# Turning a second batch by DMA transposes, and moving the next batch's loads behind its scores, in a fused attention and feed-forward kernel

## The chip, the cores and the metric

The kernel runs on one core of one Trainium2 chip. The metric is the device time of one execution in microseconds (us). "Before" is the kernel without the change, "after" the kernel with it. Because the same kernel's median moves by up to about 1 us between chips and sessions, kernels are compared by the ratio to runs of "before" that were taken in turn with them on the same chip.

In the views, PE is TensorE, PEld its weight loads, DVE is VectorE, ACT ScalarE, POOL GpSimd, and SP the engine that issues the stores and the DMA transposes; a q behind a name means that engine's sequencer. The granted clock is the share of its full clock that TensorE was allowed in a stretch. "To land" is said of a transfer whose last byte has arrived.

## The reference

```python
# q, k, v: (8, 8, 1024, 64); E, F: (64, 1024); float32 in and out
k_proj = einsum('ks,bhsd->bhkd', E, k)
v_proj = einsum('ks,bhsd->bhkd', F, v)
scores = (1 / sqrt(64)) * matmul(q, k_proj.transpose(0, 1, 3, 2))
attn   = softmax(scores)                      # over 64 projected keys
x      = matmul(attn, v_proj)                 # to (8192, 512)
g      = x @ w_gate                           # (8192, 1536)
out    = (g * sigmoid(g) * (x @ w_val)) @ w_out
```

## The kernel before

All large matmuls are bf16. The work is cut into 8 batches of 2 chunks of 512 tokens. A chunk has 12 steps; a step is a gate group (`gps`), a value group (`vps`) and an output group (`yps`) of four 512-wide matmuls each. The attention of the *next* batch is placed between these groups, in numbered slots, two to a step. A unit of attention in a slot is for instance the projection of k and v (`u_KV`), a score group (`u_S`), its sum and reciprocal on VectorE (`u_R`), its multiply on GpSimd (`u_N`), or a product with the projected values (`u_PV`).

Scores need q turned, and the products with v need the attention turned. A turn is either four TensorE transposes and a copy (`u_T`, `u_A`) or, for a whole chunk, one DMA transpose issued from SP (`u_TD`, `u_AD`):

```python
BY_DMA = [(b, ch) for b in range(1, B) for ch in range(CH)][1:]   # batches 1 to 7, but not batch 1, chunk 0
...
    def u_AD(b, ch):
        t = aw.tile([P, 4, NPAIR, P], BF16, name="AT", tag="AT")
        nc.sync.dma_start_transpose(out=..., in_=AA.pop((b, ch, "d"))...)
...
    def load_v(b, heads=(0, H)):          # fp32 in DRAM to bf16 on chip: issued by GpSimd
        ...
            nc.gpsimd.dma_start(out=t[:, h0:h1]..., in_=v[b, h0:h1]...)
```

Batches are counted from 0 in the code; "second batch" is `b == 1`, "third batch" `b == 2`.

The softmax here doesn't subtract the row's maximum and nothing guards it: scores larger than these inputs give would overflow.

## Time and profile before

| | before |
|---|---|
| median us, with the runs taken beside "after" | 573.73 (572.9 to 574.41, 4 runs) |
| span of the profiled execution | 572.4 us |
| TensorE share of the chain that ended last | 94% |
| first feed-forward group starts | 22.57 us |
| steps 12 and 24 start (the first `gps` of the second and third chunk; the second batch's attention lies mostly between them) | 47.72 and 87.03 us |

The prediction shows the lines of the page that carry this. In short: TensorE works almost without a hole from 22.57 us to the end, so time is won only by taking instructions off TensorE, by starting sooner, and it is lost wherever TensorE has to wait.

The third batch's projection, in the timeline of TensorE in the kernel before (start us, us, what):

```profile
87.03 1.03 PE L322 MATMUL gps<-xT,wg 128*128 128x512 bf16 x4
...
88.45 0.38 PE L147 MATMUL kvp<-vb,FT 128*64 128x512 bf16 x1
...
90.06 1.04 PE L322 MATMUL vps<-xT,wv 128*128 128x512 bf16 x3
```

The projection runs from 88.21 to 90.06, 1.85 us.

### The profile page before, as it was taken

What the parts mean: (1) busy time and instruction counts of PE and PEld (TensorE: products, weight loads), DVE (VectorE), ACT (ScalarE), POOL (GpSimd) and SP (SyncE); (2) the same over time, 40 slices, a digit from 0 to 9 for tenths busy, and PEclk for the clock granted to TensorE, in tenths of its full rate; (3) what the DMA queues carried; (4) which work ended last, traced back from release to release, by engine and by line L of the source; (5) the groups of instructions that cost most, each with busy time, mean ns of one, the idle gap of its engine ahead of it and who ended that gap; (6) DMA issues with size and microseconds to landing.
All of it is one profiled execution on the core that took longest, in us unless ns stands there. A gap on an engine that the chain in (4) does not pass through costs nothing.

```text
span 572.4 us, 7867 instructions
## 1 busy us (share of the span) xinstructions
PE 561.2 (98%) x2910; PEld 268.6 (47%) x2967; DVE 336.8 (59%) x580; ACT 237.0 (41%) x416; POOL 107.9 (19%) x121
## 2 busy tenths in 40 slices
PE   8899999999999999999999999999999999999997
PEld 4654544444444444444444444444444444444444
DVE  2787566666466744766556665567546674554550
ACT  1655444353425434444335434354342543443232
POOL 6734131234002400124001330023200220000000
PEclk9999999999999999999999999999999999999999
DMA  9999993539901698037951399204990124100012
GB/s 160 196 200 206 201 161 74 93 64 196 201 37 41 110 190 157 18 75 129 187 108 38 59 179 195 63 22 88 197 176 37 42 52 74 38 37 25 31 39 92
DMA packets 105927, 61.34 MB, mean 107 GB/s; under 512 B 58016, under 2 KB 97696, under 8 KB 105888
## 3 DMA queue, kind: packets, MB, share of 16 engines
q0 software_dynamic: 42288, 29.89, 36.1%
q1 hardware_dynamic: 63312, 30.68, 25.1%
q8 instruction: 23, 0.38, 0.3%
q10 hardware_dynamic: 288, 0.26, 0.1%
q14 instruction: 16, 0.13, 0.1%
HBM read 60.29 MB, written 16.78 MB: 135 GB/s over the span
## 4 chain that ended last, share of the span: by engine, by line
PE 94%; DMA 2%; POOL 1%; ACT 1%; issue 1%; DVE 0%; POOLq 0%
PE yps L360 29%; PE vps L322 29%; PE gps L322 29%; PE kvp L147 3%; PE sc L227 2%; DMA vb<-in_v_dram 2%; PE pv L285 2%; PE aTp L274 0%; ACT xT L135 0%; PE qTp L193 0%; POOL kb L88 0%; PE kTp L172 0%; POOL qb L107 0%; ACT th L334 0%; PE pv L300 0%
## 5 line engine op out<-in xcount | busy, mean ns | idle before, releaser
L341 DVE SCALAR_TENSOR_TENSOR s<-th,gps 128x512 f32<-128x512 f32 x192 | 130.5, 680 | 138.0 <-ACT th L334 137.8
L322 PE MATMUL gps<-xT,wg 128*128 128x512 bf16 (+1 forms) x755 | 195.7, 377 | 1.2
L322 PE MATMUL vps<-xT,wv 128*128 128x512 bf16 (+1 forms) x761 | 195.9, 377 | 0.8
L360 PE MATMUL yps<-wo,hT 128*128 128x512 bf16 (+2 forms) x761 | 191.5, 376 | 0.8
L334 ACT ACTIVATE th<-gps 128x512 f32<-128x512 f32 x192 | 114.6, 597 | 162.6 <-PE gps L322 155.1
L346 DVE TENSOR_TENSOR hT<-s,vps 128x512 bf16<-128x512 f32 x192 | 132.0, 688 | 22.1 <-PE vps L322 1.5
L360 PEld LDWEIGHTS <-hT 128*128 128x128 bf16 x780 | 76.2, 98 | 89.9
L258 POOL TENSOR_TENSOR AAd<-ee,rr 128x512 bf16<-128x512 f32 x52 | 54.1, 1040 | 319.5 <-issue 168.4
L322 PEld LDWEIGHTS <-wv 128*128 128x128 bf16 x776 | 73.9, 98 | 82.9 <-issue 3.3
L322 PEld LDWEIGHTS <-wg 128*128 128x128 bf16 x776 | 74.0, 98 | 81.3 <-issue 0.6
L370 ACT ACTIVATE ysb<-yps 128x512 f32<-128x512 f32 (+1 forms) x65 | 38.4, 590 | 78.1 <-PE yps L360 74.4
L135 ACT CAST xT<-pv 128x512 bf16<-128x512 f32 x62 | 36.1, 585 | 51.3 <-PE pv L285 50.3
L242 DVE TENSOR_REDUCE zz<-ee 128x8 f32<-128x512 f32 x64 | 43.5, 679 | 17.9 <-ACT ee L231 17.9
L231 ACT ACTIVATE ee<-sc 128x512 f32<-128x512 f32 x64 | 37.9, 595 | 17.4 <-PE sc L227 17.4
L285 PE MATMUL pv<-AT,BDV 128*128 128x512 bf16 x60 | 22.6, 379 | 0.1
L227 PEld LDWEIGHTS <-qTd 128*128 128x128 bf16 x208 | 16.0, 98 | 12.3
L227 PE MATMUL sc<-BD,qTd 128*128 128x128 bf16 x208 | 20.1, 219 | 0.1
L135 DVE CAST BDV<-kvp 64x256 bf16<-64x256 f32 x14 | 6.0, 426 | 22.1 <-ACT ks L157 19.1
L258 POOL TENSOR_TENSOR AA<-ee,rr 128x512 bf16<-128x512 f32 x10 | 10.3, 1038 | 35.2 <-DVE rr L244 33.6
L147 PE MATMUL kvp<-kb,ET 128*64 128x512 bf16 (+1 forms) x72 | 15.5, 357 | 1.3 <-DMA kb<-in_k_dram 1.3
L244 DVE RECIPROCAL rr<-zz 128x8 f32<-128x8 f32 x64 | 13.0, 203 | 6.2
L147 PE MATMUL kvp<-vb,FT 128*64 128x512 bf16 (+1 forms) x72 | 15.5, 358 | 1.0 <-DMA vb<-in_v_dram 1.0
(49 smaller groups left out, 144.8 us busy)
## 6 DMA issues: line engine op xcount, KB each, us to landing
out_dram<-ysb SPq DMA_DIRECT2D x63, 256.0 KB, 2.3
qb<-in_q_dram POOLq DMA_DIRECT2D x15, 512.0 KB, 16.6
kb<-in_k_dram POOLq DMA_DIRECT2D x7, 1024.0 KB, 11.6
vb<-in_v_dram POOLq DMA_DIRECT2D x7, 1024.0 KB, 14.2
wo<-in_moe_w_out_dram POOLq DMA_DIRECT2D x2, 768.0 KB, 14.8
wg<-in_moe_w_gate_dram POOLq DMA_DIRECT2D x5, 256.0 KB, 10.4
wv<-in_moe_w_val_dram POOLq DMA_DIRECT2D x5, 256.0 KB, 10.4
kb<-in_k_dram POOLq DMA_DIRECT2D x2, 512.0 KB, 8.7
```

Of the source, the lines that this page charges most:

```text
L135: (nc.scalar.copy if eng is nc.scalar else eng.tensor_copy)(out=out, in_=in_)
L147: nc.tensor.matmul(out=t[lo : lo + 64, h0:h1].rearrange("p h d -> p (h d)"), lhsT=w[:, j, :], rhs=src[b][:, h0:h1, j, :], start=(j == 0), ...
L227: nc.tensor.matmul(out=ps[:, n, :], lhsT=t[:, n, :], rhs=BD[b % 2][:, 4 * g + n, :], start=True, stop=True)
L231: nc.scalar.activation(out=e[:].rearrange("p h j k -> p (h j k)"), in_=ps[:].rearrange("p a k -> p (a k)"), func=AF.Exp, scale=scale,)
L242: nc.vector.reduce_sum(out=z[:], in_=e[:], axis=AX.X)
L258: eng.tensor_tensor(out=a.rearrange("p j h k -> p h j k"), in0=ee.pop((b, u))[:], in1=rr.pop((b, u))[:].unsqueeze(3).to_broadcast([P, 4, 2 ...
L322: nc.tensor.matmul(out=ps[:, ts], lhsT=(wg, wv)[w][:, kt, f * P : (f + 1) * P], rhs=x[:, kt, ts], start=(kt == 0), stop=(kt == NKT - 1),)
L334: nc.scalar.activation(out=th[:], in_=ps[:], func=AF.Tanh, scale=0.5)
L341: nc.vector.scalar_tensor_tensor(out=s1[:], in0=th[:], scalar=1.0, in1=g[:], op0=ALU.add, op1=ALU.mult)
L346: nc.vector.tensor_tensor(out=hT[c][:, f, :], in0=s1[:], in1=ps[:], op=ALU.mult)
L360: nc.tensor.matmul(out=yy[c][:, cs], lhsT=hT[c][:, f, i * P : (i + 1) * P], rhs=wo[:, f, cs], start=(f == 0), stop=(f == NFT - 1),)
L370: nc.scalar.activation(out=ysb[:, cs], in_=yy[c][:, cs], func=AF.Copy, scale=0.5)
```

## The change

The intent, as the diff reads, is threefold: turn the second batch's first chunk by DMA as well, so that TensorE has eight transpose groups fewer; start sooner; and, to keep the new DMA transposes clear of loads, issue the third batch's loads later, behind the second batch's scores. The diff, cut to its core:

```diff
-BY_DMA = [(b, ch) for b in range(1, B) for ch in range(CH)][1:]
+BY_DMA = [(b, ch) for b in range(1, B) for ch in range(CH)]
 ...                                  # load_k, load_v, load_q: parts by head or by token
     def place(b):
         if b == 1:
-            put(30, u_TD, 1, 1)
-            put(34, u_KV, 1, "k")
-            put(36, u_KT, 1)
-            put(40, u_KV, 1, "v")
-            sa = (37, 38, 39, 40, 48, 50, 52, 54)
-            tt = (35, 36, 37, 38)
-            ta = (41, 42, 43, 44)
-            put(57, u_AD, 1, 1)
-            sp = (43, 44, 45, 46, 66, 67, 68, 69)
+            put(22, u_TD, 1, 0)
+            put(29, u_KV, 1, "k")
+            put(32, u_KT, 1)
+            put(40, u_KV, 1, "v")
+            sa = (36, 37, 38, 39, 43, 44, 45, 47)
+            put(42, u_AD, 1, 0)
+            put(30, u_TD, 1, 1)
+            put(50, u_AD, 1, 1)
+            sp = (45, 45, 46, 46, 66, 67, 68, 69)
         else:
-            put(s0, u_KV, b)                     # s0 = 48 for the third batch
-            put(s0 + 3, u_KT, b)
-            o = 14 if b == 2 else 6
-            put(s0 + (3 if b == 2 else -6), u_TD, b, 0)
-            put(s0 + (5 if b == 2 else -4), u_TD, b, 1)
+            put(s0 + (8 if b == 2 else 0), u_KV, b)
+            put(s0 + (11 if b == 2 else 3), u_KT, b)
+            o = 13 if b == 2 else 6
+            put(s0 + (9 if b == 2 else -6), u_TD, b, 0)
+            put(s0 + (11 if b == 2 else -4), u_TD, b, 1)
 ...
         for b in range(2, B):
-            s0 = 48 * (b - 1) - (12 if b == 2 else 24)      # third batch: slots 36, 38, 40, 42
+            s0 = 48 * (b - 1) - (20 if b == 3 else 24)
+            at = (46, 47, 48, 48) if b == 2 else (s0, s0 + 2, s0 + 4, s0 + 6)
 ...  # the start
-        load_k(0, 0, 4)
+        kraw = [...]                  # first half of k as fp32 through ACT's queue, cast on VectorE
+        for i in range(2):
+            nc.scalar.dma_start(out=kraw[i][:], in_=k[0, 2 * i : 2 * i + 2]...)
 ...
-        load_k(0, 4, 8)
-        load_q(0, 0, 2)
-        load_v(0, (0, 4, 8))
+        load_q(0, 0, (0, 2))
+        load_k(0, 4, 8)
+        load_q(0, 0, (2, 4))
+        load_v(0, (0, 4, 6, 8))
         load_w_gv(0, 1)
-        load_w_gv(1, 2)
-        load_w_gv(2, 4)
+        load_w_gv(1, 2, (0,))
 ...                                   # one score group with its multiply on GpSimd
+        load_w_gv(1, 2, (1,))
 ...                                   # two more multiplies
+        load_w_gv(2, 4)
 ...                                   # further loads and copies reordered
```

Within a slot the loads come first.

## The prediction

> **What bounds the kernel now.** I read the page's busy table first, then the chain that ended last, then the chain in order of time for the first 25 us, then the timeline of TensorE (PE) from 20 to 95 us, and last the table of stretches.
>
> ```profile
> PE 561.2 (98%) x2910; PEld 268.6 (47%) x2967; DVE 336.8 (59%) x580; ACT 237.0 (41%) x416; POOL 107.9 (19%) x121
> ...
> PE 94%; DMA 2%; POOL 1%; ACT 1%; issue 1%; DVE 0%; POOLq 0%
> ```
>
> The first line is busy time by engine, the second the shares of the chain that set the end. PE is the bound. The busy 98% alone would not say so, because the warm-up matmuls on zeros and modelled ends are in it; the chain does: 94% of the span is PE work that follows PE work. The 2% of DMA is one piece near the start:
>
> ```profile
> 6.18 13.83 DMA vb<-in_v_dram
> 20.05 1.07 PE kvp L147 x8
> ```
>
> (start us, us, what). The second half of the first batch's v lands at 20.0 us and releases its projection. The first real feed-forward matmul is the `gps` line of the PE timeline:
>
> ```profile
> 22.57 0.73 PE L322 MATMUL gps<-xT,wg 128*128 128x256 bf16 x4
> ...
> 34.65 0.39 PE L193 MATMUL qTp<-ident_bf,qb 128*128 128x128 bf16 x4
> 34.87 1.03 PE L322 MATMUL vps<-xT,wv 128*128 128x512 bf16 x4
> ```
>
> The last two lines price a group of four PE transposes: it starts at 34.65, the next group at 34.87, so it costs PE 0.22 us, not the printed 0.39 (that is a modelled latency). A four-matmul 512-wide group starts every 0.865 us (28.61, 29.47, 30.33, 31.20 in the same view).
>
> So the span has three parts: a start of 22.57 us; PE work without a hole from there to 569.2, which is 546.7 us; a tail of 3.2 us. As a check I summed the middle: 2304 feed-forward matmuls x 0.216 = 498.1; 60 score groups x 0.217 = 13.0; about 62 PV matmuls, 13.4; projections 3.5 + 6 x 1.85 = 14.6; 16 transpose groups x 0.22 = 3.5; 7 key transposes, 1.5: 544.1 us. Only about 2.6 us of bubbles are left. The change can win only by fewer PE instructions or an earlier start. The start is bound by transfers:
>
> ```profile
> 0.00:5.00 5.00, 3.81 (x11) 1.32 (x11) 1.79 (x5) 1.28 (x1) 3.81 (x12) 1.00 0.55 124
> 5.00:10.00 5.00, 3.83 (x26) 2.67 (x26) 0.85 (x2) 0.74 (x2) 3.45 (x6) 1.00 1.11 160
> 10.00:15.00 5.00, 4.18 (x34) 2.42 (x33) 1.77 (x8) 1.32 (x3) 2.21 (x3) 1.00 1.35 201
> 15.00:20.00 5.00, 3.65 (x41) 2.72 (x41) 4.19 (x11) 4.04 (x9) 2.54 (x3) 1.00 1.40 197
> ```
>
> (stretch, length, busy of PE, PEld, DVE, ACT, POOL, clock, DMA share, GB/s written.) From 10 us on the DMA engines move about 200 GB/s, counted in bf16 as it lands; before that they are under-used. They stay near 200 until 75 us (198 to 207 in each stretch of 5), then fall to 161 and 127.
>
> **What the Trainium skill says.** (1) "TensorE: Matmul & The Clock Gate", section "Wait — 56ns, not 53.3ns?": warm back-to-back matmuls start every 215.7 ns at 512 columns. The trace agrees: 0.865/4 = 0.216 us. (2) "DMA: Bandwidth & Descriptors", section "Issuing engines are not separate DMA queues": loads from several queues share the same 16 DMA engines, only issue time is saved. This caps the gain of moving half of k to ACT's queue; the trace shows that early there is spare rate to fill (124 and 160 against 200). (3) Same page, "Queues, rings and completion order": each DMA engine takes turns between queues by packet, so a DMA transpose slows a load beside it. The trace agrees in kind: transposes of 512 KB land in a median of 5 us but up to 17 us. (4) "SBUF — State Buffer", section "SBUF: two separate sides": a VectorE fp32 copy within SBUF can lock GpSimd out while it writes descriptors. The new casts of k on DVE are such copies; the kernel before has none, so its trace cannot tell.
>
> **The change, part by part.**
>
> 1. *All turns of the second batch by DMA.* Its first chunk loses four groups of q transposes and four groups of attention transposes on PE: 8 x 0.22 = **1.76 us** off PE, all on the path, since PE has no holes there. Eight copies leave ACT and DVE, which are not the bound. Added: two DMA transposes. One has its q well ahead. The attention one is tight. I walked the new slots with the PE costs above: the last scores of the chunk at about 67.5 us, then exp 0.6, sum and reciprocal 0.9, multiply 1.04, so its input is ready at about 70.5; the first PV that needs it comes at about 78.5. There are 8 us for a landing of about 5, if no load is in flight.
>
> 2. *Third batch's loads behind the scores.* This keeps those 8 us clear: before, its 3 MB ran until about 80 us; now they are issued from about 79.5 us, behind the multiplies on GpSimd. Cost: slack. k needs 5 us at 200 GB/s, v 5 more, the two q 2.5 each, with 2 us of latency and a transpose in between; v lands at about 93 to 96, its projection (moved 8 slots later) comes at about 94.6. The first q transpose can start at about 97 and land at 102 to 105; its scores come at about 103.6. I expect 0 to 2.5 us of new PE wait, **0.9 us** on average.
>
> 3. *Start.* Half of k goes as fp32 through ACT's queue (issued at about 0.7 us instead of GpSimd's 1.25), E on SP and F on ACT at once; q's first quarter goes ahead of k's second half; v's last piece is a quarter. Bytes needed before the last v are the same: k, q and v are 2.5 MB as bf16, E and F cost about 0.25 MB in the same measure. Before, the first 10 us moved 0.62 + 0.80 MB; less the fp32 discount, about 1.17 MB. Saturated at 0.2 MB/us from 2.2 us it would be 1.56 MB: at most 2 us to win. GpSimd's own loads start later (its identity masks are now first)[...], so I take 1.4 us. The chain after the last v was 22.57 - 20.05 = 2.5 us. Now the projection is half as long (0.6 against 1.07 us) but on ACT an attention copy stands ahead of the xT copy (0.59 us each): no gain. One PV2 group more lies ahead of the first feed-forward matmul: 0.2 us of later work is gone. Start gain: **1.6 us**. Fewer warm-up matmuls (19 against 23) and eight more small v projections lie beside the wait for DMA and count for nothing.
>
> 4. *Weights and later loads reordered.* wo comes after the next q and k, 1.5 MB or about 7.5 us later: from about 46 to 52 us. It is first used at about 56. No cost expected, but it is a margin of only 3 or 4 us.
>
> Sum: 1.76 + 1.6 - 0.9 = 2.5 us, and I add 0.5 for bubbles that go with the transposes (at 44.9 to 48.8 the chain leaves PE for ACT copies). 574.05 - 3.0 = **571.0 us**.
>
> **The rivals.** *(a) A wait in place of the transposes.* For: the third batch's loads have about 1 us of margin, and v loads took 12 to 25 us from issue to landing in the first 70 us. Against: much of that was queueing, and the loads were visibly re-timed together with the projection (8 slots). If it bites twice, 3 us are lost: about 573.5. *(b) GpSimd starves the early weights.* The third weight pair (blocks 2 and 3) is now issued behind three multiplies, at about 17 us by my walk against 13.9 before, and is needed about 4 us after the first feed-forward matmul. For: landings of 8 to 13 us. Against: the queue is shorter then. Cost 0 to 2 us. *(c) The start is worth the full 2 us and more and nothing waits:* 574.05 - 1.76 - 3 - 0.5 = 568.8. *(d) The start is hidden anyway:* if v still lands at 20 us because the total bytes are equal, only the transposes count: about 572. An engine that becomes the new bound is not in sight: DVE is at 59%.
>
> **Range and chances.** The sure part is 1.76 us; the start adds 0 to 3.5, waits take 0 to 3. Range 568.6 to 573.0. Two per cent is 11.5 us: the whole start before the weights is only 22.57 us and PE work is fixed, so faster by 2% is at 0.01. Slower by 2% needs a stall of over 14 us: 0.01.
>
> **What would show each step.** PE with 55 fewer instruction rows in total (weight loads included) and no `qTp` or `aTp` group between 50 and 95 us; the last piece of v landing at 18 to 19 us and the first `gps` at about 21; the attention transpose of the second batch landing before its PV at about 78; the third batch's `kvp` starting within a microsecond of the end of the PE instruction before it. The prediction is wrong if the first `gps` comes before 19 us or after 22.5, if the chain of waits shows a DMA of batch two or three of over 3 us between 50 and 110 us, or if weights hold PE at 24 to 40 us.

## More of the kernel before

The loads of k, v and q cast on the way. They are issued by GpSimd **in program order with GpSimd's multiplies** (`u_N`): a load that stands behind a multiply in the program can't be issued before that multiply's inputs exist.

## The result, and the profile after

The changed kernel took **577.88 us** (577.04 to 577.97, 4 runs) against 573.73 of the kernel before in the same rounds: ratio 1.007, with a 95% interval of 1.0052 to 1.0087. Ratios here and below are the mean time of one kernel's runs over that of the other's in the same rounds, so not quite the quotient of the medians. It is 4 us slower instead of 3 us faster: still within 2%, but above the predicted range of 568.6 to 573.0.

The page of the changed kernel has these two lines where the prediction quotes those of the kernel before (busy time by engine; shares of the chain that ended last):

```profile
PE 565.6 (98%) x2939; PEld 267.6 (46%) x2939; DVE 334.8 (58%) x577; ACT 236.5 (41%) x417; POOL 109.1 (19%) x122
...
PE 89%; DMA 4%; DVE 2%; POOL 2%; ACT 1%; issue 1%; DVEq 0%; POOLq 0%; ACTq 0%
```

The busy share still says 98% and would mislead. The chain says that TensorE now carries 89% of the span instead of 94, and that DMA, VectorE and GpSimd carry the difference. The list of TensorE's waits (us in total, times, longest) has one that is new and large:

```profile
PE kvp L149 <- DMA vb<-in_v_dram: 4.3, 1, 4.3
```

The timeline of TensorE shows where, and a second loss behind it (start us, us, what, and in brackets the idle time with what ended it):

```profile
94.98 1.03 PE L324 MATMUL gps<-xT,wg 128*128 128x512 bf16 x4
...
100.66 0.58 PE L149 MATMUL kvp<-vb,FT 128*64 128x512 bf16 x1 [4.32 <-DMA vb<-in_v_dram]
...
101.04 0.63 PE L149 MATMUL kvp<-vb,FT 128*64 128x512 bf16 x1
101.47 0.63 PE L149 MATMUL kvp<-vb,FT 128*64 128x512 bf16 x1
...
104.16 1.50 PE L324 MATMUL vps<-xT,wv 128*128 128x512 bf16 x4
105.50 1.03 PE L362 MATMUL yps<-wo,hT 128*128 128x512 bf16 x4
```

The third batch's projection waits for v until 100.66. Then its matmuls come 0.43 us apart, where the kernel before has 0.216, and the next group takes 105.50 - 104.16 = 1.34 us instead of 0.865. So the wait is followed by some 4.5 us at half clock. The table of stretches shows both, and also that the transfers began late (stretch, length, busy of PE, PEld, DVE, ACT, POOL with counts, granted clock, a DMA share that isn't used here, GB/s):

```profile
80.00:85.00 5.00, 5.00 (x31) 2.44 (x29) 3.40 (x7) 3.44 (x7) 3.41 (x5) 1.00 0.08 8
85.00:90.00 5.00, 5.00 (x24) 2.25 (x23) 3.12 (x6) 1.87 (x4) 3.56 (x4) 1.00 1.05 140
90.00:95.00 5.00, 5.00 (x25) 2.28 (x24) 2.57 (x5) 1.79 (x3) 0.00 (x0) 1.00 1.19 219
95.00:100.00 5.00, 1.34 (x6) 0.38 (x5) 0.56 (x1) 0.60 (x1) 0.00 (x0) 0.83 1.24 193
100.00:105.00 5.00, 4.34 (x18) 1.77 (x18) 0.12 (x1) 0.58 (x1) 0.00 (x0) 0.50 1.32 210
```

From 80 to 85 us the DMA engines are all but idle, at 8 GB/s. Then they run, and TensorE stands still for most of 95 to 100 all the same. The clock is 1.00 until 95 and 0.50 after 100; in stretches of 1 us it falls at about 98.3, while TensorE still waits. Why the loads were late is in the chain in order of time (start us, us, what):

```profile
78.13 0.70 DVE zz L244
...
79.13 0.56 DVE s L343
...
79.78 0.69 DVE hT L348
80.47 0.61 DVE zz L244
...
81.87 0.44 POOL AAd L260
...
82.86 0.41 POOL kb L88
...
83.81 0.99 POOL AAd L260
84.80 15.81 DMA vb<-in_v_dram
100.62 0.04 issue
100.66 3.57 PE kvp L149 x15
```

(The lines on `rr`, the reciprocal after each sum, and on pauses between instructions are left out.) Read it upward from the last line. The projection waits for v, which takes 15.8 us from its issue at 84.80. Its issue waits on GpSimd for a multiply (83.81), which stands behind the issue of k (82.86), which stands behind another multiply (81.87). That one waits for a sum on VectorE (`zz`, 80.47), and the sum stands in VectorE's queue behind two feed-forward products (`s`, `hT`). For the multiply at 81.87 GpSimd's own timeline names ScalarE's cast to `xT` as the releaser, not VectorE; releasers are inferred, and between the reciprocal's end at 81.4 and the multiply 0.5 us stay unexplained. Neither VectorE nor GpSimd is over 60% busy, and yet their queues set when the transfer begins.

**What the stall costs.** An undisturbed projection in the same surroundings is in experiment y2 below: from the start of the `gps` group ahead of it to the `yps` group after it are 99.42 - 95.74 = 3.68 us. Here they are 105.50 - 94.98 = 10.52. The stall costs 6.8 us. The first v matmul comes 5.68 us after that `gps` instead of 0.96: a wait of 4.7 us. The remaining 2.1 us are the half clock.

**What went as foreseen.** The stretch from the start of step 12 to that of step 24 takes 84.62 - 46.20 = 38.42 us against 87.03 - 47.72 = 39.31 before, 0.89 us less; and four score groups of 0.22 us that lay outside this stretch before lie in it now, so 0.88 us more are gone: 1.77 us. The first feed-forward group starts at 20.72 instead of 22.57.

### The profile page after: what moved, and what is told of

Same layout as the page of the kernel before. It is cut to its first block, busy times and chain, and to the rows that moved or that the text cites. A ratio compares the mean times of both kernels' runs of the same rounds, so it can differ in the third digit from the quotient of the medians. Undisturbed runs are those within 1.5% of the kernel's fastest.

```text
span 576.2 us, 7878 instructions
## 1 busy us (share of the span) xinstructions
PE 565.6 (98%) x2939; PEld 267.6 (46%) x2939; DVE 334.8 (58%) x577; ACT 236.5 (41%) x417; POOL 109.1 (19%) x122
## 4 chain that ended last, share of the span: by engine, by line
PE 89%; DMA 4%; DVE 2%; POOL 2%; ACT 1%; issue 1%; DVEq 0%; POOLq 0%; ACTq 0%
PE yps L362 28%; PE vps L324 26%; PE gps L324 26%; PE kvp L149 3%; DMA vb<-in_v_dram 3%; PE sc L229 2%; PE pv L287 2%; DMA wv<-in_moe_w_val_dram 2%; PE warm L464 1%; DVE zz L244 1%; POOL AA L260 0%; DVE hT L348 0%; DVE s L343 0%; POOL wg L117 0%; ACT xT L137 0%
## 5 line engine op out<-in xcount | busy, mean ns | idle before, releaser
L324 PE MATMUL gps<-xT,wg 128*128 128x512 bf16 (+1 forms) x776 | 197.8, 377 | 0.3
L324 PE MATMUL vps<-xT,wv 128*128 128x512 bf16 (+1 forms) x776 | 198.0, 378 | 0.1
L362 PE MATMUL yps<-wo,hT 128*128 128x512 bf16 (+1 forms) x780 | 194.5, 376 | 0.0
L260 POOL TENSOR_TENSOR AAd<-ee,rr 128x512 bf16<-128x512 f32 x56 | 58.2, 1041 | 350.2 <-issue 157.2
L229 PEld LDWEIGHTS <-qTd 128*128 128x128 bf16 x224 | 17.2, 98 | 13.2
L149 PE MATMUL kvp<-vb,FT 128*64 128x512 bf16 (+2 forms) x80 | 17.3, 362 | 4.6 <-DMA vb<-in_v_dram 4.3
L229 PE MATMUL sc<-BD,qTd 128*128 128x128 bf16 x224 | 21.6, 219 | 0.0
L149 PE MATMUL kvp<-kb,ET 128*64 128x512 bf16 (+1 forms) x72 | 17.2, 383 | 0.2 <-DMA kb<-in_k_dram 0.2
L107 POOL DMA_DIRECT2D qb<-in_q_dram x17 | 15.5, 913 | 0.6 <-DMA wv<-in_moe_w_val_dram 0.6
## 6 DMA issues: line engine op xcount, KB each, us to landing
qb<-in_q_dram POOLq DMA_DIRECT2D x15, 512.0 KB, 17.8
vb<-in_v_dram POOLq DMA_DIRECT2D x7, 1024.0 KB, 14.4
```

Source lines behind the costliest of these rows:

```text
L149: nc.tensor.matmul(out=t[lo : lo + 64, h0:h1].rearrange("p h d -> p (h d)"), lhsT=w[:, j, :], rhs=src[b][:, h0:h1, j, :], start=(j == 0), ...
L229: nc.tensor.matmul(out=ps[:, n, :], lhsT=t[:, n, :], rhs=BD[b % 2][:, 4 * g + n, :], start=True, stop=True)
L260: eng.tensor_tensor(out=a.rearrange("p j h k -> p h j k"), in0=ee.pop((b, u))[:], in1=rr.pop((b, u))[:].unsqueeze(3).to_broadcast([P, 4, 2 ...
L324: nc.tensor.matmul(out=ps[:, ts], lhsT=(wg, wv)[w][:, kt, f * P : (f + 1) * P], rhs=x[:, kt, ts], start=(kt == 0), stop=(kt == NKT - 1),)
L362: nc.tensor.matmul(out=yy[c][:, cs], lhsT=hT[c][:, f, i * P : (i + 1) * P], rhs=wo[:, f, cs], start=(f == 0), stop=(f == NFT - 1),)
```

## The experiments

The theory: the changed kernel is slow by the stall alone, 4.6 us of waiting for v and 2.1 us of half clock after it; the transposes' 1.8 us are won. Rivals: the DMA transposes are slow wherever the loads lie (so the loads' place only chooses which wait there is); the half clock is a minor matter and the wait all; the start isn't worth what its first group shows.

All results, each against the kernel before of its own rounds:

| run | edit against the changed kernel | median us | ratio to before, 95% |
|---|---|---|---|
| changed kernel | none | 577.88 | 1.007 (1.0052 to 1.0087) |
| r1 | none, again | 577.80 | 1.0074 (1.0062 to 1.0086) |
| x1 | third batch's loads in their old slots | 585.75 | 1.0205 (1.016 to 1.0251) |
| x2 | 20 matmuls on zeros ahead of the projection | 576.95 | 1.0067 (1.0052 to 1.0082) |
| x3 | second attention transpose 8 slots later | 576.11 | 1.0048 (1.0029 to 1.0067) |
| x4 | projection and scores 4 slots later | 579.48 | 1.011 (1.0095 to 1.0125) |
| y1 | loads one slot earlier, in one block | 576.60 | 1.0049 (1.0037 to 1.0061) |
| y2 | y1 and x3 together | 571.24 | 0.9965 (0.9954 to 0.9977) |
| y2, again | the same | 571.59 | 0.997 (0.9956 to 0.9984) |
| z1 | new start alone, all else as before | 573.34 | 1.000 (0.9987 to 1.0012) |
| b1 | y2, and the third weight pair issued earlier | 570.60 | 0.9953 (0.994 to 0.9967) |

All of them gave correct results.

### x1: the loads where they were

```diff
-            at = (46, 47, 48, 48) if b == 2 else ...
+            at = (36, 38, 40, 42) if b == 2 else ...
```

> The changed kernel with one thing undone: the third batch's loads stand at slots 36 to 42 again instead of 46 to 48. Theory L (the loss is the wait of the third batch's projections for its v, because the load is issued at 84.8 us for a use at 96): v lands before 96, no wait there, no fall of the clock, 571.0 us (6.8 below the changed kernel). Rival C (the loads were moved because they collide with the second batch's attention transpose, issued at 74.8 us and used at 80.1): that transpose lands 3 to 8 us late, PE waits before the first PV of the second batch, and the time is 574 to 578.

Measured: 585.75 us, in two clusters (583.0 and 583.4, 588.1 and 589.2); the trace is of the slowest, 589.2. Rival C is right in kind and too small in size. The wait for v is gone, and two worse ones have come. The waits of TensorE, then the issue queue of SP, in x1:

```profile
PE pv L287 <- DMA AT<-AAd: 8.0, 1, 8.0
PE sc L229 <- DMA qTd<-qb: 4.2, 1, 4.2
```

```profile
75.42 11.00 SPq L214 DMA_TRANSPOSE AT<-AAd  x1
```

In the changed kernel the same transpose is issued at 74.84 with the DMA engines nearly free:

```profile
74.84 1.94 SPq L214 DMA_TRANSPOSE AT<-AAd  x1
88.59 7.23 SPq L214 DMA_TRANSPOSE AT<-AAd  x1
```

Its issue holds SP's queue for 1.9 us when quiet and 11.0 us beside the loads of v and q; in x1 it lands 20.2 us after its issue, and its product is due some 5 us after its issue (80.08 - 74.84 in the changed kernel). The second line is the *other* attention transpose of the changed kernel: it lies beside the third batch's loads and holds SP's queue for 7.2 us, landing after 15.9. So the loads had to move: with all turns by DMA, the old place costs some 8 us more than the new one. The conflict is between DMA transposes and loads, and the place of the loads chooses who waits; y2 shows a place where nobody does.

### x2: keep TensorE busy while it waits

```diff
+            if b == 2:
+                put(s0 + 8, warm, 20)                   # 20 matmuls of zeros, 4.4 us
             put(s0 + (8 if b == 2 else 0), u_KV, b)
```

> The changed kernel plus 20 matmuls on zeros (4.3 us of PE work at 0.216 us) just before the projections that wait for v. Nothing else moves and v lands when it landed before (about 100.6). Theory G (the wait of 4.6 us also drops the PE clock to half for some 6 us, which costs 2.2 us on top: projections 3.6 us instead of 1.85, next group 1.34 instead of 0.87): the clock stays at full speed and the kernel takes 575.7. Rival W (the wait alone is the cost, the clock is read wrongly): the filler only fills the wait, 577.9, no change.

Measured: 576.95 us, ratio 1.0067 against 1.007 of the changed kernel; the profiled execution's span is 575.3 against 576.2. The timeline of TensorE in x2:

```profile
96.03 4.48 PE L466 MATMUL warm<-zeros 128*128 128x512 bf16 x20
...
101.48 0.38 PE L149 MATMUL kvp<-vb,FT 128*64 128x512 bf16 x1 [0.64 <-DMA vb<-in_v_dram]
...
104.18 1.03 PE L362 MATMUL yps<-wo,hT 128*128 128x512 bf16 x4
```

The clock stays at 1.00 in every stretch of 2 us, and from the first v matmul to the next `yps` it is 2.70 us, not the 105.50 - 100.66 = 4.84 of the changed kernel. So the half clock is worth **2.1 us at this place**, and it comes from the idle time alone: the same data, waits and transfers without idleness have no half clock. Over the whole span the gain is only about 1 us in the profiled execution and not to be told from zero in the timed runs, so the 575.7 that theory G expected was missed. v landed 0.8 us later here, and the next turned q then came late (a wait of 0.3 us); it may be that the half clock partly delays work that would wait anyway, but no run separates that. A filler is no cure.

### x3: the second attention transpose after the loads

```diff
-            put(50, u_AD, 1, 1)
+            put(58, u_AD, 1, 1)
```

> The changed kernel with the attention transpose of the second batch's second chunk issued behind the first q transpose of the third batch (slot 58 instead of 50), so that it no longer shares the DMA engines with v. Theory S (sharing makes v late: 0.5 MB at 0.2 to 0.3 MB/us): v lands 2 us earlier, near 98.5, the wait is under 3 us, the clock may not fall, 571.5 to 575.5. Theory L in its strict form (only the issue time matters): v lands within 0.7 us of 100.6 and the time stays at 577.5 to 578.

Measured: 576.11 us, between what the two theories expected. The four runs are 574.46 and 575.9 to 576.6, and the profiled execution is the fastest of them, so its trace shows a lucky case. In it v lands 14.4 us after its issue instead of 15.8, TensorE waits 2.9 us for it and the clock doesn't fall. Taking away the transpose beside the loads is worth 1.4 us of v's landing. The other runs took 1.4 to 2.2 us more, and the record has the mean granted clock of each: 1.000 in the run with the trace, 0.996 to 0.997 in the three others. So in those the clock did fall somewhere (0.0035 of 574 us is 2 us of clock lost, or 4 us at half). Where it fell, and whether their wait was longer too, no trace shows.

### x4: the projection later instead of the loads earlier

```diff
-            put(s0 + (8 if b == 2 else 0), u_KV, b)
-            put(s0 + (11 if b == 2 else 3), u_KT, b)
-            o = 13 if b == 2 else 6
+            put(s0 + (12 if b == 2 else 0), u_KV, b)
+            put(s0 + (15 if b == 2 else 3), u_KT, b)
+            o = 17 if b == 2 else 6
```

> The changed kernel with the third batch's projections, key transposes and scores 4 slots (two steps, 5.2 us) later; loads unchanged. Theory L: v has landed by then (100.6 against about 101.2), no wait, full clock, 571.0 us, as x1. If 571 is reached here and in x1, the whole excess over the prediction is this one wait. Rival: the wait only moves to the q transpose and the scores of the third batch, 573 or more.

Measured: 579.48 us, slower still. The wait for v is gone, and this one is new among the waits of TensorE in x4:

```profile
PE pv L287 <- DMA AT<-AAd: 5.6, 1, 5.6
```

Everything of the third batch is four slots later, so its attention transpose is issued at 130.03, just behind the *fourth* batch's loads of k and v (128.58 and 129.52). It takes 18.4 us to land, and the clock is 0.50 from 146 to 150. The wait didn't go away; it moved on by one batch. What is a miss for the cure is a second case for the cause: a DMA transpose issued a few us behind 2 MB or more of a batch's loads lands in 15 to 20 us (20.2 in x1, 15.9 in the changed kernel, 18.4 here).

### y1: the loads one slot earlier

```diff
-            at = (46, 47, 48, 48) if b == 2 else ...
+            at = (45, 45, 45, 45) if b == 2 else ...
```

> The changed kernel with all four loads of the third batch at slot 45, in one block behind the multiply of the second batch's fifth score group (issue near 80.3 to 83 us): behind the attention transpose that x1 collided with, and v 3.6 us sooner than in the changed kernel. Theory P (there is a window of about 5 us with idle DMA, 80 to 85 us, that the changed kernel leaves unused): v lands near 97.5, wait about 1.5 us, no fall of the clock, 572.0 to 573.0 where the changed kernel takes 577. Rival C2 (the next attention transpose, at 88 us, slows the loads whatever their start): v lands within 1 us of where it did and the time stays above 575.5.

This puts all four load instructions right behind the fifth multiply of the batch and ahead of the sixth. k is issued at 80.27 instead of 82.86, v at 81.20 instead of 84.80. Measured: 576.60 us. The wait for v is down to 0.9 us, so the late issue is worth at least 3.4 of its 4.3 us. Most of that is given back some 10 us later, as the timeline of TensorE in y1 shows:

```profile
105.50 1.03 PE L362 MATMUL yps<-wo,hT 128*128 128x512 bf16 x4
108.85 0.40 PE L229 MATMUL sc<-BD,qTd 128*128 128x128 bf16 x4 [2.32 <-DMA qTd<-qb]
109.08 1.03 PE L324 MATMUL gps<-xT,wg 128*128 128x512 bf16 x4
109.95 1.86 PE L324 MATMUL vps<-xT,wv 128*128 128x512 bf16 x4
```

The scores wait 2.3 us for q's transpose, which now competes with what is left of the loads and the attention transpose. And at 109.95 a group takes 111.60 - 109.95 = 1.65 us: the clock fell after 2.3 us of idleness. One of the six runs took 574.9 us at a mean granted clock of 0.999, the others 576.5 to 576.7 at 0.996 to 0.997: again the runs whose clock fell are the longer ones. The 572.0 to 573.0 that theory P expected was missed by this second wait, which no theory had named. Half of the cure, then, isn't half of the gain.

### y2: both

```diff
-            put(50, u_AD, 1, 1)
+            put(58, u_AD, 1, 1)
-            at = (46, 47, 48, 48) if b == 2 else ...
+            at = (45, 45, 45, 45) if b == 2 else ...
```

> y1 and x3 together: loads at slot 45 and the second attention transpose behind the first q transpose of the third batch. Theory P with S: v lands before 96, no wait at the projections, full clock throughout, 570.5 to 571.5: what the prediction of 571.0 had assumed, and faster than the kernel before by 2.5 us or so. Rival: a new wait at the second chunk's PV or at the third batch's scores, 573 or more.

Measured: 571.24 us, and 571.59 in a second session: faster than both kernels. In the timeline of GpSimd of y2:

```profile
81.01 0.94 POOL L88 DMA_DIRECT2D kb<-in_k_dram  x1
81.94 0.88 POOL L98 DMA_DIRECT2D vb<-in_v_dram  x1
```

and in that of TensorE:

```profile
95.74 1.03 PE L324 MATMUL gps<-xT,wg 128*128 128x512 bf16 x4
...
96.70 0.40 PE L149 MATMUL kvp<-vb,FT 128*64 128x512 bf16 x1
...
99.42 1.03 PE L362 MATMUL yps<-wo,hT 128*128 128x512 bf16 x4
```

v lands at 96.5, 14.6 us after its issue, just ahead of the projection. No DMA wait of the second or third batch is left in the list, and the clock is 1.00 in all stretches of 5 us from 65 to 110. From the changed kernel to y2 the ratio falls from 1.0074 to 0.9965 in the same rounds, which is 1.09% of 573.67, or 6.3 us; the stall was counted as 6.8. That settles the cause of the excess: with the stall removed and the rest of the change kept, the kernel is faster than the one before. That it comes out at the predicted 571.0 is in part luck. The prediction's gain of 3.0 us had 0.9 of waits in it, so without waits it stood for 3.9, and y2 gains 2.0 (0.0035 of 573.67); most of the difference is the start, see z1.

> y2 (loads of the third batch at slot 45, second attention transpose behind the first q transpose of the third batch) once more, as the base for b1 on one chip: 0.9965 of the kernel before, within 0.0012.

### r1: the changed kernel again

> The changed kernel once more, as the base on this chip for the three that follow. All theories: ratio to the kernel before 1.006 to 1.008, v of the third batch lands 15 to 17 us after its issue, the PE waits 4 to 5 us and its clock falls to half.

Measured: 577.80 us; the wait for v is 4.3 us and v's landing takes 15.8 us, as in the first trace. The stall is the same in both traces, not an accident of one execution.

### z1: the new start alone

```diff
 # the start, the load functions and the loads' order of the changed kernel;
 # BY_DMA, place() and the third batch's loads of the kernel before
```

> The new start with the whole schedule after it as in the kernel before (first chunk of the second batch turned on PE, loads of the third batch at slots 36 to 42). The new start had its first feed-forward matmul 1.85 us sooner and one PV pair less behind it, and lost 0.65 us again to late weights at 31.9 to 33.2 us. Theory: 1.5 us faster than the kernel before, 0.9974 of it. Rival (weights behind more loads stall more when the rest is as before, or the start is hidden): 1.000.

Measured: 573.34 us, ratio 1.000 (0.9987 to 1.0012), so the start is worth between 0.7 us of gain and as much of loss; the rival's 1.000 came true, not the theory's 0.9974. In its trace the first feed-forward group starts at 21.50 (20.6 to 21.0 in the ten other traces with this start) against 22.57; by step 12 the lead is 46.93 against 47.72, 0.8 us. This lead is read against one trace of the kernel before, and that is of a long execution: 574.16 us, where 29 of its 31 timed runs are shorter and their median is 573.4. That would fit the whole gap; whether the extra time lies in its start, no second trace shows. y2 is 571.24 - 573.34 = -2.1 us from it, which is the body's part: 1.77 us of transposes and some 0.3 of bubbles, the latter less than the noise of the two ratios.

### b1: the third weight pair where it isn't behind multiplies

The start's lead is lost at the weights. In the stretch from 20 to 22 us the changed kernel has

```profile
20.00:22.00 2.00, 1.85 (x20) 1.54 (x18) 1.02 (x2) 1.16 (x3) 2.00 (x4) 1.00 1.41 134
```

134 GB/s where the kernel before moves 187, because GpSimd issues the third pair of weights at 18.75, behind three multiplies, instead of 13.93. Later weights come late, and TensorE waits for some at 31.6 to 33.2 us: from its first 512-wide group to the value group of step 6 the changed kernel takes 33.20 - 24.71 = 8.49 us, the kernel before 34.87 - 26.88 = 7.99, so 0.5 us are lost. In the ten traces with this order of weights, r1, z1 and both y2 among them, the loss in that stretch is 0.3 to 1.0 us, 0.7 on average.

```diff
         load_w_gv(1, 2, (1,))
+        load_w_gv(2, 4)
 ...                                  # two multiplies
-        load_w_gv(2, 4)
```

(in addition to the edits of y2)

> y2 with the third weight pair (blocks 2 and 3) issued on GpSimd ahead of its second and third multiply of the start instead of behind them (about 15.5 us instead of 18.75). The changed kernel moved only 134 GB/s in 20 to 22 us where its neighbours moved 182 and 188, some 0.1 MB less, and waited 0.65 us more for weight pairs three steps later. Theory (GpSimd starves the weight stream): the dip goes, the weights of blocks 6 and 7 land 0.5 us sooner, the waits at 31.9 to 34 us shrink by 0.5 us, 570.7 where y2 takes 571.2. Rival (total bytes bind, the dip is only re-timed): no change within 0.2 us.

Measured: 570.60 us, ratio 0.9953 against 0.997 of y2 in the same rounds. In the same stretch of b1:

```profile
20.00:22.00 2.00, 1.85 (x20) 1.66 (x19) 1.02 (x2) 1.16 (x3) 2.00 (x4) 1.00 1.57 190
```

The dip is gone, and so is the wait for weights: the stretch takes 32.58 - 24.59 = 7.99 us, as in the kernel before. Against the second trace of y2, the luckiest of the ten, b1 is 0.3 us ahead from there to the end (spans of 568.7 and 569.0). The medians differ by 1.0 us; b1's five runs lie between 570.5 and 570.8, y2's in the same rounds between 570.8 and 572.3. That number isn't sharp, as the intervals of the two ratios overlap, but it fits the 0.7 us that the other traces lose on average. b1 is the fastest version found: 2.3 us below the kernel before in its rounds.

## Why the prediction was wrong

It predicted 571.0 us and the time was 577.88. By its own steps:

- **Transposes, 1.76 us: right.** 1.77 us by the two steps' times. No `qTp` or `aTp` group lies between 50 and 95 us, and the attention transpose of the first chunk landed before its product at 80.08 without a wait, as foreseen, but with some luck: its input was ready at 74.8, not at 70.5, which left 5.2 us and not 8 for a landing of 4.3. The walk had missed the same thing as below: the last sum of the chunk stands in VectorE's queue behind a cast that waits for the projection of v, and starts at 72.63 although its exponentials were there at 69.9. The check by the number of rows is only half readable, as some matmul records of the kernel before are missing; the weight loads fell from 2967 to 2939.
- **Waits behind the third batch's loads, "0.9 us on average": this is the step that failed.** The mechanism was named, as rival (a), but its size was 6.8 us. Two terms were wrong. First, the wait was 4.7 us. The estimate had k issued at 79.5 and v landing 13.5 to 16.5 us later, at 93 to 96; k was issued at 82.86 and v landed 17.8 us later. So about 3.4 us are the late issue, and about 2.8 us, against the middle of the estimate, the slower transfer; the projection itself came 1.3 us later than estimated, which took some back. The recorded text doesn't say how it came to 79.5; the trace shows what it left out, that the multiplies ahead of k and v wait for inputs that come through VectorE's queue. The transfer was priced at 200 GB/s after 2 us of latency, with a transpose in between; DMA wrote 140 GB/s from 85 to 90 us, and the transpose was worth 1.4 us of v's landing (x3). Why those first 5 us are slow stays open. y1 and x3 measured the late issue and the transpose, y2 removed both. The second wrong term is the clock.
- **The clock: a term that was missing.** The sum had waits at their own length. A wait of 4.7 us was followed by some 4.5 us at half clock, which cost 2.1 us at this place (x2).
- **The rival's size.** Rival (a) was put at 573.5, "if it bites twice, 3 us are lost". It bit once, for 6.8 us.
- **Start, 1.6 us: mostly wrong.** v's last piece was indeed in the projection at 18.55 and the first group at 20.72, as predicted ("18 to 19", "about 21"). But z1 found 0 us, within 0.7, for the start as a whole. Rival (b), GpSimd starving the early weights, took 0.7 us of it on average over ten traces, and b1, where it takes none, confirms it. The rest of the gap between the lead in the traces, 0.8 us at step 12 in z1 and 1.5 in the changed kernel, and z1's timed runs is open; the long execution behind the one trace of the kernel before would fit it. The lock-out of GpSimd by VectorE's casts that the prediction mentions doesn't show: beside the casts at 4.49 to 5.47 us GpSimd issues the three loads of v in 2.16 us, 0.72 each, where the kernel before needs 1.51 for two.
- **Bubbles, 0.5 us: about 0.3**, as y2 and z1 differ by 2.1, though the noise is larger than that.
- **A reading:** the rate "198 to 207 in each stretch of 5" until 75 us should be 192 to 207; nothing hangs on it.
- **The later loads and wo: no cost,** right; there is no wait for it.

The sum with measured terms, from the before of the same rounds: 573.73 - 1.77 - 0.3 - 0.3 (start, by z1's medians) + 6.8 = 578.2, where 577.88 was measured. The prediction's own test, "a DMA of batch two or three of over 3 us between 50 and 110 us" in the waits, is what came true; a second one, weights that hold TensorE at 24 to 40 us, came true in small (0.5 us at 31.6 to 33.2).

## What to carry to other kernels

When loads are moved later to make room, walk to their *issue*: ask which instruction of the issuing engine stands ahead of it in program order, and where that one's inputs come from, through the queues of the other engines. Put the issues of one block of loads together, behind one instruction rather than between several, and keep a DMA transpose on neither side of them. When a wait on TensorE is possible, price it with the clock that can fall after it: here 4.7 us of wait cost 6.8 at its place. And when one of two conflicts is removed, expect the other to take over; two half cures that gave 1.3 and 1.4 us by their ratios gave over 6 together.

## What the Trainium skill lacked or had wrong

- **The fall of the clock** ("TensorE: Matmul & The Clock Gate", section "What's actually happening"): the page has an idle window of about 3.4 us that runs free of the kernel, after which the clock is half. The runs agree on the half (matmuls 0.43 us apart after the 4.7 us wait), and show that shorter idleness can do it: in the changed kernel it fell at about 98.3, 2.0 us after TensorE's last instruction; in y1 it fell at about 110, after 2.3 us of idleness and 1.1 us of work; after 2.9 us in x3's trace it didn't. So a gap shorter than the window isn't safe, and what decides between these cases is open.
- **DMA transposes beside loads** ("Advanced Engine Details and Errata", section "X-Bar Transpose (TRN2)"): the page says that transposes are as fast as regular DMAs, at 350 to 400 GB/s expected. A turn of 512 KB landed in 4.3 us here with nothing else in flight (changed kernel, issued at 74.84), and while it moved, from 76.0 to 78.4 us, DMA wrote 189 to 217 GB/s; for the plain store right behind it, from 78.4 to 79.2, DMA wrote 318 and 343. Behind a batch's loads turns landed in 15.9, 18.4 and 20.2 us (changed kernel, x4, x1). No page tells how long its issue holds SP's queue beside loads: 7.2 and 11.0 us, against 1.9 when quiet.
- **The rate of casting loads after an idle stretch** (no page has it): with k, v and q in flight DMA wrote 140 GB/s from 85 to 90 us, and 219 from 90 to 95 with a transpose beside them (changed kernel), so that the 2 MB of k and v took 17.8 us from the first issue to the last landing.
- **Program order on the issuing engine** (no page puts a cost on it): a load issued by GpSimd behind two multiplies came 3.6 us later than one placed ahead of them (84.80 against 81.20 for v), with the DMA engines at 8 GB/s meanwhile.
